# Loading the first group of q and k in fp32 over the hardware DMA queues, with the casts on VectorE and ScalarE

## Chip, cores, metric

One core of a Trainium2 chip. The metric is device time in microseconds (us) of one execution. A "span" is the same thing inside the trace, from the first to the last instruction; it is about 2 us shorter than the device time. A "fast run" is an execution that the record does not mark as slow (by its span and its granted clock, the share of the full TensorE clock that the records show); all timed runs here are fast ones, only the single run of no_norms is of unknown state.

## The reference

Cross-covariance attention over channels, followed by a gated feed-forward layer, all fp32. B, N, C = 4, 6016, 256; d_ff = 1536; tau = 1.

```python
qn = q / (np.linalg.norm(q, axis=1, keepdims=True) + 1e-06)
kn = k / (np.linalg.norm(k, axis=1, keepdims=True) + 1e-06)
s = kn.transpose(0, 2, 1) @ qn / tau          # [B, C, C], a sum over all N rows
a = softmax(s)
x = (v @ a).reshape(B * N, C)
out = (sigmoid(x @ w_gate) * (x @ w_val)) @ w_out
```

What matters here: the first output needs the scores `s` of batch 0, and these need every row of batch 0's q and k. Nothing of the main work can start before these 12.3 MB of fp32 have been read.

## The kernel before

q and k are read in groups of four row tiles (128 partitions x 4 x 256). GpSimd issues all loads, as DMAs that cast fp32 to bf16 on the way. Batch 0 has 11 full groups (0 to 10) and two small ones of two tiles and one tile, so that little is left to do after the last landing.

```python
def load_qk(b, t0, nt):
    tiles = []
    for name, src in (("q", q), ("k", k)):
        tl = qkpool.tile([P, TPC, C], BF16, tag=name, name=name + "_sb")
        nc.gpsimd.dma_start(out=tl[:, :nt, :], in_=rows(src, b)[:, t0 : t0 + nt, :])
        tiles.append(tl)
    qk[b, t0] = tiles
...
nc.scalar.preload_act_table(ACT.Sqrt)
for t0, nt in groups0[:2]:
    load_qk(0, t0, nt)
make_identity(nc, ident_bf)                   # GpSimd; cut: a second one, memsets on VectorE
for t0, nt in groups0[2:]:
    load_qk(0, t0, nt)
...
for g in range(last0 + 2):                    # the opening: batch 0's scores and norms
    if g <= last0:
        t0, nt = groups0[g]
        sq[g] = (squares(0, t0, nt, 0, nc.vector),
                 squares(0, t0, nt, 1, nc.vector if g == last0 else nc.scalar))
        for u in range(nt):
            score(0, t0, u)                   # 2 matmuls a tile: 8 for a full group
    if g >= 1:                                # column sums of the squares, 16 matmuls
        norm_mms(ps_n0, sq.pop(g - 1), groups0[g - 1][1], g == 1, g == last0 + 1)
```

After the loop come the norms, the softmax (with filler matmuls, `busy`, between them), the first products of the softmax with the weights (`ps_gh`), and then the main loop, whose first matmul is `ps_gate`.

## Time and profile before

| | before |
|---|---|
| median of the first three runs | 842.0 us (841.8 to 842.13) |
| the profiled run | 839.55 us |
| span in the trace | 837.4 us, TensorE busy 98% |
| first DMA bytes | between 2.5 and 2.6 us |
| scores of the last full group start | 32.22 us |
| first `ps_gate` matmul | 40.09 us |

The last two rows split the span: up to the last full group the DMA sets the pace, from there to `ps_gate` a chain of short steps on all engines, and after `ps_gate` TensorE. That last part is the same in every trace: span minus the start of the first `ps_gate` matmul is 797.2 to 797.6 us in all 14 of them. So whatever a variant does to the span is already visible at about 40 us.

### The profile page before, as it was taken

The page shows a single profiled execution, that of the slowest core. Times are in us where ns is not written, and L with a number is a line of the kernel's source. Part 1 is how long each engine was busy: PE and PEld are TensorE (multiplying, and loading weights), DVE is VectorE, ACT ScalarE, POOL GpSimd, SP SyncE. Part 2 cuts the span into 40 slices and gives each one's busy share as a digit, 9 for nine tenths or more (in the row PEclk, how much of TensorE's full clock was granted, in tenths as well). Part 3 has the DMA queues.
Part 4 walks back from the last instruction along what each step waited for, and adds up shares of the span by engine and source line. Part 5 has one row for each costly group of instructions (what it writes and reads, how often), then busy time and mean ns, then how long its engine had stood idle before and what let it go on. Part 6 is the DMA issues. An engine that isn't in the chain of part 4 may idle for free.

```text
span 837.4 us, 13986 instructions
## 1 busy us (share of the span) xinstructions
PE 816.6 (98%) x5327; PEld 506.3 (60%) x5338; DVE 565.3 (68%) x976; ACT 389.3 (46%) x639; POOL 83.9 (10%) x161
## 2 busy tenths in 40 slices
PE   5899999999999999999999999999999999999998
PEld 4546666665666666665566666666566565656666
DVE  2477777776667777777656777777766666666664
ACT  3554444446544444444554444444654444444442
POOL 5532100002011100000210020000000000000000
PEclk9899999999999999999999999999999999999999
DMA  9999624227655543223864353223222522322211
GB/s 176 206 206 188 131 51 89 61 51 142 119 102 107 101 108 63 48 51 89 150 136 86 88 117 78 51 76 67 58 48 51 95 51 76 76 48 68 48 35 69
DMA packets 78738, 76.65 MB, mean 92 GB/s; under 512 B 50768, under 2 KB 55632, under 8 KB 78672
## 3 DMA queue, kind: packets, MB, share of 16 engines
q0 software_dynamic: 24208, 39.33, 28.4%
q1 hardware_dynamic: 54464, 36.45, 15.8%
q8 instruction: 41, 0.67, 0.3%
q14 instruction: 25, 0.20, 0.1%
HBM read 78.64 MB, written 24.64 MB: 123 GB/s over the span
## 4 chain that ended last, share of the span: by engine, by line
PE 91%; DMA 3%; DVE 2%; ACT 1%; issue 1%; POOL 0%; ACTq 0%; POOLq 0%
PE ps_o L88 29%; PE ps_gate L88 28%; PE ps_val L88 28%; PE ps_s L88 4%; DMA k_sb<-in_k_dram 3%; PE ps_gh L88 2%; DVE hT L344 1%; ACT g_sb L343 1%; PE ps_rk L88 0%; ACT gh_H L299 0%; DVE out_sb L370 0%; PE ps_n L88 0%; DVE gh_G L301 0%; DVE gh_H L301 0%; DVE x_sb L246 0%
## 5 line engine op out<-in xcount | busy, mean ns | idle before, releaser
L344 DVE TENSOR_TENSOR hT<-ps_val,g_sb 128x512 bf16<-128x512 f32 (+1 forms) x576 | 390.9, 679 | 220.1 <-ACT g_sb L343 216.2
L343 ACT ACTIVATE g_sb<-ps_gate 128x512 bf16<-128x512 f32 (+1 forms) x576 | 338.6, 588 | 400.0 <-PE ps_gate L88 387.6
L88 PE MATMUL ps_val<-vT,gh_H 128*128 128x512 bf16 (+1 forms) x1152 | 338.1, 375 | 0.5
L88 PE MATMUL ps_gate<-vT,gh_G 128*128 128x512 bf16 (+1 forms) x1152 | 337.5, 375 | 0.5
L88 PE MATMUL ps_o<-w_out_sb,hT 128*128 128x256 bf16 x2256 | 326.1, 273 | 0.0
L88 PEld LDWEIGHTS <-hT 128*128 128x128 bf16 x2256 | 220.7, 98 | 124.8
L88 PEld LDWEIGHTS <-gh_H 128*128 128x128 bf16 x1152 | 112.7, 98 | 132.9 <-ACT gh_H L299 1.5
L88 PEld LDWEIGHTS <-gh_G 128*128 128x128 bf16 x1152 | 112.4, 98 | 37.3 <-ACT gh_G L299 0.3
L370 DVE COPY out_sb<-ps_o 128x256 f32<-128x256 f32 x188 | 78.0, 415 | 20.9 <-PE ps_o L88 20.9
L106 POOL DMA_DIRECT2D v_sb<-in_v_dram x48 | 25.5, 531 | 631.3 <-DMA vT<-v_sb 496.3
L88 PE MATMUL ps_s<-k_sb,q_sb 128*128 128x256 bf16 x376 | 72.3, 295 | 12.2 <-DMA k_sb<-in_k_dram 12.2
L88 PEld LDWEIGHTS <-q_sb 128*128 128x128 bf16 x376 | 39.1, 104 | 20.3 <-issue 7.5
L162 DVE TENSOR_TENSOR sq<-q_sb 128x1024 bf16<-128x1024 bf16 (+3 forms) x46 | 30.4, 661 | 25.3 <-PE ps_n L88 19.1
L200 DVE TENSOR_TENSOR acc<-acc,sq 128x1024 bf16<-128x1024 bf16 (+1 forms) x66 | 44.1, 669 | 0.0
L97 POOL DMA_DIRECT2D k_sb<-in_k_dram x49 | 26.9, 549 | 14.5 <-DMA k_sb<-in_k_dram 9.1
L97 POOL DMA_DIRECT2D q_sb<-in_q_dram x49 | 26.8, 548 | 13.7 <-DMA q_sb<-in_q_dram 6.3
L162 DVE TENSOR_TENSOR sq<-k_sb 128x1024 bf16<-128x1024 bf16 (+2 forms) x34 | 22.4, 658 | 0.0
L160 ACT ACTIVATE sq<-k_sb 128x1024 bf16<-128x1024 bf16 (+1 forms) x12 | 12.2, 1021 | 20.1 <-DMA k_sb<-in_k_dram 19.7
L88 PE MATMUL ps_gh<-w_gate,e_sb 128*128 128x512 bf16 x41 | 12.8, 378 | 1.6 <-DVE rrow L274 1.2
L88 PEld LDWEIGHTS <-e_sb 128*128 128x128 bf16 x112 | 9.9, 97 | 6.8 <-issue 3.2
L88 PE MATMUL ps_gh<-w_val,e_sb 128*128 128x512 bf16 x44 | 13.2, 379 | 0.4
L299 ACT ACTIVATE gh_G<-ps_gh,rrow 128x512 bf16<-128x512 f32 x12 | 8.2, 687 | 9.7 <-PE ps_gh L88 5.6
(44 smaller groups left out, 99.7 us busy)
## 6 DMA issues: line engine op xcount, KB each, us to landing
out_dram<-out_sb SPq DMA_DIRECT2D x44, 512.0 KB, 2.9
q_sb<-in_q_dram POOLq DMA_DIRECT2D x44, 256.0 KB, 6.7
k_sb<-in_k_dram POOLq DMA_DIRECT2D x44, 256.0 KB, 7.6
v_sb<-in_v_dram POOLq DMA_DIRECT2D x44, 256.0 KB, 3.9
out_dram<-out_sb SPq DMA_DIRECT2D x4, 384.0 KB, 2.4
w_gate<-in_moe_w_gate_dram POOLq DMA_DIRECT2D x3, 256.0 KB, 7.0
w_val<-in_moe_w_val_dram POOLq DMA_DIRECT2D x3, 256.0 KB, 7.6
w_out_sb<-in_moe_w_out_dram POOLq DMA_DIRECT2D x1, 768.0 KB, 13.0
```

Of the source, the lines that this page charges most:

```text
L88: nc.tensor.matmul(out, lhsT=lhsT, rhs=rhs, start=start, stop=stop, **kw)
L97: nc.gpsimd.dma_start(out=tl[:, :nt, :], in_=rows(src, b)[:, t0 : t0 + nt, :])
L106: nc.gpsimd.dma_start(out=v_sb[:, :nt, :], in_=rows(v, b)[:, t0 : t0 + nt, :])
L160: nc.scalar.activation(out=sq[:, :nt, :], in_=src[:, :nt, :], func=ACT.Square)
L162: engine.tensor_tensor(out=sq[:, :nt, :], in0=src[:, :nt, :], in1=src[:, :nt, :], op=ALU.mult)
L200: nc.vector.tensor_tensor(out=acc[:, :nt, :], in0=acc[:, :nt, :], in1=st[b]["sq", w][:, :nt, :], op=ALU.add)
L299: nc.scalar.activation(out=dst, in_=ps, func=ACT.Copy, scale=r)
L343: nc.scalar.activation(out=g_sb[:, :n], in_=ps_gate[:, :n], func=ACT.Sigmoid)
L344: nc.vector.tensor_tensor(out=hts[b, ci][:, f, :n], in0=ps_val[:, :n], in1=g_sb[:, :n], op=ALU.mult)
L370: nc.vector.tensor_copy(out=out_sb[:, s, :], in_=ps)
```

## The change

Intent: SP and ScalarE should be able to issue a DMA earlier than GpSimd does, and the first bytes should then move earlier. No cast is asked of these DMAs (the prediction says on what ground), so group 0 lands in fp32 tiles and is cast by VectorE (q) and ScalarE (k).

```diff
+    t0, nt = groups0[0]
+    qk[0, 0] = [qkpool.tile([P, TPC, C], BF16, tag=n, name=n + "_sb") for n in ("q", "k")]
+    first_f32 = [consts.tile([P, nt, C], FP32, name=f"first{w}") for w in range(2)]
+    for eng, tl, src in zip((nc.sync, nc.scalar), first_f32, (q, k)):
+        eng.dma_start(out=tl, in_=rows(src, 0)[:, t0 : t0 + nt, :])
     nc.scalar.preload_act_table(ACT.Sqrt)
-    for t0, nt in groups0[:2]:
-        load_qk(0, t0, nt)
+    load_qk(0, *groups0[1])
 ...
+    nc.vector.tensor_copy(out=qk[0, 0][0], in_=first_f32[0])
+    nc.scalar.copy(qk[0, 0][1], first_f32[1])
     for t0, nt in groups0[2:]:
         load_qk(0, t0, nt)
```

## The prediction

> **What bounds the kernel now.** I read the page first, then the chain of waits cut to the first 34 us, then the opening as a timeline, then stretches of it as a table. The page settles where a change to the opening can count at all. The chain that ended last is:
>
> ```profile
> PE 91%; DMA 3%; DVE 2%; ACT 1%; issue 1%; POOL 0%; ACTq 0%; POOLq 0%
> PE ps_o L88 29%; PE ps_gate L88 28%; PE ps_val L88 28%; PE ps_s L88 4%; DMA k_sb<-in_k_dram 3%; PE ps_gh L88 2%; DVE hT L344 1%; ACT g_sb L343 1%; PE ps_rk L88 0%; ACT gh_H L299 0%; DVE out_sb L370 0%; PE ps_n L88 0%; DVE gh_G L301 0%; DVE gh_H L301 0%; DVE x_sb L246 0%
> ```
>
> TensorE carries 91% of the span. The DMA share, 3% (about 27 us of 837.4), is the loading of batch 0's q and k, at the front. The chain cut to the opening shows that this is one unbroken wait for k:
>
> ```profile
> 5.06 6.56 DMA k_sb<-in_k_dram
> ...
> 11.91 10.48 DMA k_sb<-in_k_dram
> ...
> 22.67 9.51 DMA k_sb<-in_k_dram
> 32.18 0.04 issue
> 32.22 1.03 PE ps_s L88 x8
> ```
>
> Columns are start, length, what. The reader is to see that until 32.2 us the end is set by one thing, when the last full k group lands. From there on it is TensorE's own work, so a change of x us in that landing should pass almost undiminished to the end. Everything else in the opening has slack. The stretches show why the landing comes when it does (stretch, its length, busy time of PE, PEld, DVE, ACT and POOL, granted clock, DMA share, GB/s written):
>
> ```profile
> 2.25:2.50 0.25, 0.00 (x0) 0.00 (x0) 0.00 (x0) 0.00 (x0) 0.25 (x2) 1.00 0.00 0
> 2.50:2.75 0.25, 0.00 (x0) 0.00 (x0) 0.00 (x0) 0.00 (x0) 0.25 (x1) 1.00 1.30 82
> 2.75:3.00 0.25, 0.00 (x0) 0.00 (x0) 0.00 (x0) 0.00 (x0) 0.25 (x2) 1.00 1.15 57
> 3.00:3.25 0.25, 0.00 (x0) 0.00 (x0) 0.00 (x0) 0.00 (x0) 0.25 (x1) 1.00 0.61 41
> 3.25:3.50 0.25, 0.00 (x0) 0.00 (x0) 0.00 (x0) 0.00 (x0) 0.25 (x2) 1.00 0.42 57
> 3.50:4.00 0.50, 0.00 (x0) 0.00 (x0) 0.00 (x0) 0.00 (x0) 0.42 (x2) 1.00 0.95 164
> 4.00:4.50 0.50, 0.00 (x0) 0.00 (x0) 0.00 (x0) 0.00 (x0) 0.43 (x3) 1.00 1.11 209
> ```
>
> No data moves before 2.5 us, there is a weak first microsecond, and from 4.0 us on the engines are saturated. The 209 GB/s are bf16 bytes written; the sources are fp32, so they read 418 GB/s. A group of q and k is 2 x 512 KiB of fp32, so 1.049 MB / 418 GB/s = 2.51 us. The score matmuls of successive groups start at 9.22, 11.67, 14.23 and 16.67 us, 2.48 us apart: the rate of the source bytes sets the pace. The timeline of the first group:
>
> ```profile
> 1.23 0.66 POOL L97 DMA_DIRECT2D q_sb<-in_q_dram  x1 [0.78 <-POOLq L494]
> 5.43 0.69 DVE L162 TENSOR_TENSOR sq<-q_sb 128x1024 bf16<-128x1024 bf16 x1 [4.42 <-DMA q_sb<-in_q_dram]
> 6.63 1.06 ACT L160 ACTIVATE sq<-k_sb 128x1024 bf16<-128x1024 bf16 x1 [4.61 <-DMA k_sb<-in_k_dram]
> 6.65 1.86 PE L88 MATMUL ps_s<-k_sb,q_sb 128*128 128x256 bf16 x8 [6.65 <-DMA k_sb<-in_k_dram]
> ```
>
> q is issued at 1.23 us, its first bytes move at 2.5, it lands at 5.4, and k at 6.6.
>
> **What the Trainium skill says, and whether the trace agrees.** (1) "DMA: Bandwidth & Descriptors", section "SWDGE vs HWDGE vs iDMA": a DMA that casts must be issued from GpSimd; plain ones may go from SP or ACT. That is why the change needs an fp32 tile and two casts. Its Specifications give a first-byte latency of about 1 us for the GpSimd path and 0.6 us for the other. The trace has 1.27 us from the start of the first GpSimd issue to first bytes; for the hardware path it has only the output stores, 512 KB each, 2.9 us from issue to landing. (2) The same page, "Issuing engines are not separate DMA queues": all DMAs share 16 engines and interleave, so more issuers save issue time alone. The flat 209 GB/s agrees with one shared limit. (3) "VectorE: DVE Perf Modes", "The perf-mode tier table": an fp32 copy in SBUF runs at two elements a cycle, 1227 ns for 2048. An estimate from that page's fixed 150 cycles: (150 + 512) / 0.96 = 0.69 us for 1024. Nothing in the trace before is such a copy. (4) "ScalarE: Activation LUTs", "What ACT_TABLE_LOAD costs": 186 ns + 0.833 ns an element, 1.04 us for 1024; the trace's square of that size takes 1.06 us.
>
> **The change, part by part.** *Removed*: two GpSimd issues, 0.66 + 0.54 us, and group 0's 1.05 MB from the GpSimd queue. Group 1 takes its place at 1.23 us. GpSimd's issues (0.55 us for 1.25 us of transfer) run ahead of the data, so the saving there is worth nothing by itself.
>
> *Added, start of the stream*: SP and ACT issue at about 0.75 us (ACT's first instruction, the table load, starts at 0.74, so ACT is free then). An issue on SP takes 0.33 to 0.36 us in the trace, and a 512 KB store lands 2.9 us after it starts: less 1.25 us of transfer (0.524 MB / 418 GB/s) leaves 1.65 us, of which I put 0.85 ahead of the data and 0.8 behind, a choice. Data should therefore move from about 1.6 us in place of 2.5. What counts is the effective start at full rate. Before: k of group 0 landed at 6.63; less the 2.51 us for two tiles and an assumed 0.6 us of completion, 3.5 us. After: 1.6 us plus a weak spell as in the table (there 1.0 us) gives 2.6; a shorter one gives down to 2.1. The stream should thus end 0.9 to 1.4 us earlier; I take 1.1.
>
> *Added, the casts*: 0.69 us on VectorE and 1.04 us on ScalarE, beside each other. The three queues share the engines from about 2.6 us on, so group 0 loses its head start: of its 1.05 MB some 0.2 move by then, and 0.85 MB at two thirds of 418 GB/s take 3.0 us, plus completion 6.2 us at the latest; served alone, about 4.9. I take 5.9. ScalarE's cast then ends near 6.95, so the first score starts about 7.0, 0.3 us later than the 6.65 of before. This is not on the path that sets the end, for a group costs a slow TensorE about 2.27 us against 2.51 us of arrival (1.86 for scores plus 0.61 for norms, partly overlapped), and 1.57 when fast. A backlog under a microsecond is gone well before 32 us. ScalarE's square at 1.06 us and VectorE's at 0.69 us leave more slack.
>
> *Moved*: the table load falls behind ACT's issue, some 0.4 us, and its result is first needed at 35 us. The fp32 tiles take 8 KB a partition, no cost in time.
>
> *Sum*: the last full k lands at about 31.1 us in place of 32.2. Of the 1.1 us I expect to lose up to 0.2 because of TensorE's clock. These stretches are the reason:
>
> ```profile
> 17.90:24.60 6.70, 3.45 (x67) 3.05 (x65) 2.08 (x3) 2.11 (x2) 2.64 (x5) 0.99 1.12 210
> 24.70:31.40 6.70, 6.18 (x58) 4.53 (x58) 1.38 (x2) 3.17 (x3) 3.01 (x6) 0.51 1.12 208
> 31.60:38.00 6.40, 5.81 (x105) 5.09 (x102) 3.73 (x11) 4.01 (x6) 5.25 (x8) 1.00 1.24 204
> ```
>
> The granted clock is half from about 24.7 to 31.5 us and full just before the tail. If that change stays at the same moment, work that arrives at 31.1 runs for 0.4 us at half speed. The gain is then 0.9 to 1.1 us, and 842.0 becomes about 841.0.
>
> **Rivals.** *Nothing gained, the start was hidden*: if the hardware queues' first bytes were as late as GpSimd's, or the weak microsecond came from cold memory and were only moved, the total bytes would decide. For it: rates are equal on all queues, and the first stretches have packets in flight (share 1.30) with few bytes arriving. Against it: the share falls to 0.42 at 3.25 us, so the engines were short of work there, which a second source fills. Time: 842.0.
>
> *The cast becomes the bound*: the chain of landing, cast, square and score delays group 0 and this is never made up. For it: one cold group fills 2.27 of 2.51 us. Against it: the 17.9 to 24.6 stretch has 3.45 us of work in 6.7, so there is room to catch up. Time: 842.3 to 842.8.
>
> *The clock phases shift*: TensorE gets its full clock in one stretch and loses it in the next. A later start followed by denser work could move the half-clock stretch onto the tail, where from 32.2 to 38 us nearly all is TensorE or what waits for it. The eight scores took 1.86 us slow against 1.03 fast; over the tail that makes 2 to 3 us. For it: a half-clock stretch follows one with 51% work. Against it: the kernel puts filler matmuls (ps_busy) into the tail to prevent this. Time: 843 to 844. I give it one chance in eight.
>
> *More than I think*: if the loads start at full rate at once, the effective start is 1.6 us and the gain near 1.9: 840.1.
>
> **Range and chances.** The centre is 841.0. Below, 840.1 is the best rival; above, a lost phase makes 843.5. The chip's spread, 0.3 us in the three runs, is small beside these, but another chip may differ by a microsecond or so. I set 839.3 to 843.2 for eight times in ten. Two per cent is 16.8 us. The whole opening up to the last landing is 32 us and 27 of them are source bytes that must move either way, so no part of this change can win or lose that: same 0.985, faster 0.005, slower 0.01.
>
> **What would show each step right or wrong.** In the changed kernel's stretches, bytes should move by about 1.6 us. First score near 7.0 us, cast 0.7 us on VectorE and 1.04 on ScalarE. Later groups should be ready about 1.1 us earlier and 2.5 us apart, the scores after the last full k at about 31.1, and the first ps_gate matmul about 1 us before its 40.09 of before. I am wrong if the first bytes come at 2.5 us again, if TensorE no longer waits for k in the opening (the cast took over), if the tail runs at half clock, or if the last landing comes earlier but the end does not.

## The result, and the profile after

The changed kernel takes 839.42 us (838.86 to 840.19, 6 runs), the kernel before 841.4 us over its own 6 runs (839.72 to 842.13). Ratio 0.998, 95% interval 0.9967 to 0.9993, "same" at two per cent. Ratios here are the mean time of one kernel's fast runs over that of the other's of the same rounds, so not quite the ratio of the medians.

The first thing to see is a contradiction: the profiled run of the changed kernel has the *longer* span, 838.0 us against 837.4, although its runs are faster. Part of the answer is which executions were profiled: the trace before is of a run of 839.55 us, faster than all six timed runs (839.72 is the lowest), and the trace after is of the slowest of its six (840.19). The two traces must be taken apart before either is believed.

**The start went as hoped.** The timeline of the changed kernel (start, length, engine, instruction, in brackets the idle time before it and what ended it):

```profile
0.74 0.40 ACTq L114 DMA_DIRECT2D first<-in_k_dram  x1
0.74 0.39 SPq L114 DMA_DIRECT2D first<-in_q_dram  x1
1.23 0.67 POOL L97 DMA_DIRECT2D q_sb<-in_q_dram  x1 [0.78 <-POOLq L501]
5.54 0.69 DVE L127 CAST q_sb<-first 128x1024 bf16<-128x1024 f32 x1 [4.53 <-DMA first<-in_q_dram]
5.75 1.04 ACT L128 CAST k_sb<-first 128x1024 bf16<-128x1024 f32 x1 [3.29 <-DMA first<-in_k_dram]
6.84 3.57 PE L88 MATMUL ps_s<-k_sb,q_sb 128*128 128x256 bf16 x16 [6.84 <-ACT k_sb L128]
```

The loads go out 0.49 us ahead of GpSimd's first. The casts take 0.69 and 1.04 us, and the last line holds 16 matmuls, two groups in one piece: group 1 was already there when group 0 was done. In stretches (the last columns are granted clock, DMA share, GB/s written):

```profile
1.50:2.00 0.50, 0.00 (x0) 0.00 (x0) 0.00 (x0) 0.50 (x1) 0.50 (x2) 1.00 0.76 90
2.50:2.75 0.25, 0.00 (x0) 0.00 (x0) 0.00 (x0) 0.00 (x0) 0.17 (x2) 1.00 0.39 147
3.00:3.25 0.25, 0.00 (x0) 0.00 (x0) 0.00 (x0) 0.00 (x0) 0.18 (x3) 1.00 1.02 377
5.50:6.00 0.50, 0.00 (x0) 0.00 (x0) 0.46 (x1) 0.25 (x1) 0.50 (x2) 1.00 1.08 205
```

Bytes move in the stretch from 1.5 us. (The packet records have the first packet of q or k at 1.76 us, and at 2.59 in the kernel before.) While the fp32 tiles are written the rate shows as near 400 GB/s, as source and destination have the same size; at 5.5 us it is back at the 205 of casting DMAs. One thing went otherwise than predicted: GpSimd's loads of group 1 are issued at 1.23 us, as before, but their first packet moves at 4.97 us, when the fp32 loads are nearly done (their last packet ends at 5.34). In all eight traces with early hardware loads GpSimd's first packet comes at 4.80 to 5.29 us, in the others at 2.59 to 2.62. No run tests why. The engines are full at 3.0 us, where in the kernel before they were full at 4.0.

**A part of the lead is lost at group 6 in this pair of traces.** The score matmuls of groups 5, 6 and 7, first of the kernel before:

```profile
19.25 1.03 PE L88 MATMUL ps_s<-k_sb,q_sb 128*128 128x256 bf16 x8 [0.72 <-DMA k_sb<-in_k_dram]
...
22.43 1.03 PE L88 MATMUL ps_s<-k_sb,q_sb 128*128 128x256 bf16 x8 [1.77 <-DMA k_sb<-in_k_dram]
...
24.74 1.86 PE L88 MATMUL ps_s<-k_sb,q_sb 128*128 128x256 bf16 x8 [0.90 <-DMA k_sb<-in_k_dram]
```

and of the changed kernel:

```profile
18.22 1.75 PE L88 MATMUL ps_s<-k_sb,q_sb 128*128 128x256 bf16 x8 [1.11 <-DMA k_sb<-in_k_dram]
...
21.59 1.86 PE L88 MATMUL ps_s<-k_sb,q_sb 128*128 128x256 bf16 x8 [1.22 <-DMA k_sb<-in_k_dram]
...
24.14 1.54 PE L88 MATMUL ps_s<-k_sb,q_sb 128*128 128x256 bf16 x8 [0.28 <-DMA k_sb<-in_k_dram]
```

Group 5 is 1.03 us earlier than before. Group 6 comes late in both kernels (3.18 and 3.37 us after its predecessor, where 2.5 is the rule), and by group 7 the lead is 0.60 us. It stays there: the last full group starts at 31.61 against 32.22. Two checks show that the stream as a whole loses nothing. In the packet records 3 MB of the source have been read at 10.66 us before and 9.89 after, and 11 MB at 29.85 and 29.06: the lead is 0.77 and 0.79 us. (A casting DMA's packet records count bf16 bytes; they are doubled here.) And in the second pair of traces, below, the lead is 0.98 us at group 5 and 0.92 at group 9. What differs at group 6 is how late the last packet of a group comes.

**The tail is slower in this one trace.** The chain that ended last, from the last full group on, before:

```profile
32.22 1.03 PE ps_s L88 x8
33.26 0.38 PE ps_n L88 x16
33.63 0.52 PE ps_s L88 x4
...
40.25 0.43 PE ps_gate L88 x2
```

and after:

```profile
31.61 1.86 PE ps_s L88 x8
33.48 0.40 PE ps_n L88 x16
33.88 0.88 PE ps_s L88 x4
...
40.95 0.43 PE ps_gate L88 x2
```

The same eight score matmuls take 1.86 us, not 1.03, and the next four 0.88, not 0.52. From the last full group's scores to the first `ps_gate` matmul it takes 9.18 us (31.61 to 40.79) against 7.87 (32.22 to 40.09; the chain leaves out what overlaps the piece before, so it has `ps_gate` 0.16 us later than the timeline). The stretch says why:

```profile
31.60:38.00 6.40, 6.29 (x89) 5.23 (x89) 3.04 (x10) 3.31 (x5) 4.94 (x7) 0.70 1.24 205
```

The granted clock is 0.70 in it; before it was 1.00 (shown in the prediction). In this execution TensorE ran at half clock from 28.6 to 35.4 us. So the sum of this pair of traces is -0.61 us of stream and +1.31 us of tail, together the +0.7 us by which `ps_gate` starts later. Whether the change causes the slow tail or chance does is the question for the experiments.

### The profile page after: what moved, and what is told of

It is laid out like the page before. It is cut to its first block, busy times and chain, and to the rows that moved or that the text cites. A ratio compares the mean times of both kernels' runs of the same rounds, so it can differ in the third digit from the quotient of the medians.

```text
span 838.0 us, 14001 instructions
## 1 busy us (share of the span) xinstructions
PE 817.0 (97%) x5338; PEld 506.6 (60%) x5338; DVE 566.3 (68%) x977; ACT 390.6 (47%) x640; POOL 83.2 (10%) x159
## 4 chain that ended last, share of the span: by engine, by line
PE 91%; DMA 3%; DVE 2%; ACT 1%; issue 1%; POOL 0%; ACTq 0%; POOLq 0%
PE ps_o L88 29%; PE ps_gate L88 28%; PE ps_val L88 28%; PE ps_s L88 4%; DMA k_sb<-in_k_dram 3%; PE ps_gh L88 2%; DVE hT L351 1%; ACT g_sb L350 1%; PE ps_rk L88 0%; DVE out_sb L377 0%; ACT gh_H L306 0%; PE ps_n L88 0%; DVE gh_H L308 0%; DVE gh_G L308 0%; DVE x_sb L253 0%
## 5 line engine op out<-in xcount | busy, mean ns | idle before, releaser
L88 PEld LDWEIGHTS <-q_sb 128*128 128x128 bf16 x376 | 39.1, 104 | 20.8 <-issue 7.1
```

What stands on the lines that cost most here:

```text
L88: nc.tensor.matmul(out, lhsT=lhsT, rhs=rhs, start=start, stop=stop, **kw)
```

## The experiments

Theory A: the gain is the earlier start of the byte stream; the casts are hidden; where TensorE's half-clock stretches fall is chance, a matter of the single execution. Rivals: B, the change moves the clock's phase; C, the earlier stream is lost elsewhere; D (an addition to A), the late group is the work of an instruction fetch, a DMA packet that brings TensorE its next instructions; E, DMAs that don't cast, or the hardware queues as such (E'), are the gain; F, the casts cost; G, GpSimd's queue is the slow part.

Twelve kernels ran in three batches of four, each batch on a chip of its own. So times are compared within a batch, or by the ratio to the runs of the kernel before in the same batch. Their results are in one table. "First bytes" is the first packet of q or k in the packet records and "11 MB" the time at which 11 MB of the source have been read; "group 9" and "`ps_gate`" are the starts, in the trace, of that group's scores and of the first `ps_gate` matmul.

| batch | run | first bytes | 11 MB | group 9 | `ps_gate` | median us (lowest to highest of 5) | ratio to before |
|---|---|---|---|---|---|---|---|
| 0 | before | 2.59 | 29.85 | 29.75 | 40.09 | 841.4 (839.72 to 842.13, 6 runs) | |
| 0 | after | 1.76 | 29.06 | 29.15 | 40.79 | 839.42 (838.86 to 840.19, 6 runs) | 0.9980 |
| 1 | before_copy | 2.60 | 29.88 | 30.11 | 40.44 | 839.99 (839.87 to 841.54) | 0.9991 |
| 1 | after_copy | 1.76 | 28.98 | 29.19 | 40.00 | 839.40 (838.98 to 840.22) | 0.9984 |
| 1 | fill_before | 2.59 | 30.00 | 30.18 | 40.90 | 840.19 (840.03 to 840.36) | 0.9990 |
| 1 | fill_after | 1.75 | 29.10 | 29.23 | 39.88 | 839.04 (839.00 to 839.29) | 0.9977 |
| 2 | wide_before | 2.59 | 29.83 | 29.97 | 40.87 | 840.37 (839.91 to 840.48) | 0.9994 |
| 2 | wide_after | 1.75 | 29.04 | 29.25 | 39.60 | 838.83 (838.63 to 839.39) | 0.9979 |
| 2 | wide_pool_f32 | 2.62 | 29.92 | 30.22 | 40.60 | 839.84 (839.44 to 840.33) | 0.9989 |
| 2 | wide_act_late | 1.77 | 29.08 | 29.54 | 39.87 | 838.91 (838.76 to 839.32) | 0.9978 |
| 3 | wide_late_hw | 2.60 | 29.97 | 30.01 | 40.92 | 840.00 (839.49 to 840.20) | 0.9983 |
| 3 | wide_cast_twice | 1.75 | 29.03 | 29.06 | 40.03 | 839.21 (839.13 to 839.71) | 0.9976 |
| 3 | wide_two_groups | 1.76 | 29.11 | 29.14 | 40.05 | 839.56 (839.26 to 839.84) | 0.9979 |
| 3 | no_norms | 1.75 | 28.98 | 28.37 | 40.19 | 839.57 (1 run) | |

The column "11 MB" falls into two sets: 28.98 to 29.11 us wherever the first bytes come at 1.75 to 1.77, and 29.83 to 30.00 wherever they come at 2.59 to 2.62. In both sets it hardly depends on who issues, on casts, or on fillers.

### The two kernels again (before_copy, after_copy)

No edit. The kernel before:

> The kernel before against itself, for the noise and for a second trace of it. Theory A (the half-clock stretch of TensorE falls at a different phase in each run, and the two profiles of before and after differ in the tail only by that): the runs' mean granted clocks are not all 0.996; they spread over 0.990 to 0.997 and the spans over some 1.5 us; in this trace the scores of the last full group start at 32.2 us within 0.3 us, whatever the clock. Rival B (the phase follows the kernel and the change moved it): all runs near 0.996 and the half-clock stretch again at 24.7 to 31.5 us. Ratio 1.000 either way.

And the changed one:

> The changed kernel again, for a second trace and a clean ratio. Theory A: k of group 1 is ready near 8.2 us (1.0 us before the kernel before), last full group's scores at 31.2 to 31.6 us, the tail at full or half clock by chance; ratio 0.9985 to 0.9995 (0.4 to 1.3 us). Rival B: the half-clock stretch is again at 28.6 to 35.4 us, so the tail from the last full group's scores to the first ps_gate matmul takes 9.3 us again against 8.0 of before, and the ratio is 1.000 to 1.001.

The copy of the kernel before measured 0.9991 of the kernel before (interval 0.9979 to 1.0004): the same program, and the medians of five and nine runs differ by 1.0 us. That is the size of the effect looked for, so plain timing of these kernels hardly resolves it. The clock moved: in the copy of before the half-clock stretch reaches from 21.4 to 31.6 us (24.4 to 31.3 in the first trace), in the copy of after the later of two lies at 26.0 to 32.8 (28.6 to 35.4 in the first). Rival B, a phase that the kernel fixes, is out. That the change makes a bad phase likelier is not excluded by two traces of each, but the runs show no sign of it: the mean granted clock is 0.992 both over 32 runs of the kernel before and over 11 of the changed one. The tails follow the clock: 7.85 us in the copy of before (32.59 to 40.44), 8.35 us in that of after (31.65 to 40.00) with the half clock covering its first microsecond. The mean granted clocks of the before runs in this batch go from 0.987 to 0.996, so they spread, as A expects, even a little further. One part missed: the last full group of the copy starts at 32.59, 0.37 us off the first trace, just outside the 0.3 I had allowed. It is not the stream: 11 MB are read within 0.03 us of each other, and up to group 5 (19.25 and 19.22) the traces agree. They part at group 6 (22.43 and 22.57), behind the fetch at 20.2 us, which costs the one 0.5 us for good and the other 0.9. In the copy of after the last full group starts at 31.65, and the ratio is 0.9984, each just outside its expected range.

### TensorE kept busy (fill_before, fill_after)

```diff
+    busy(48)                                   # 128 columns each
     for g in range(last0 + 2):
         if g <= last0:
+            if 1 <= g and groups0[g][1] == TPC:
+                busy(12)
```

> The kernel before with filler matmuls on TensorE while it waits: 48 ahead of the first group and 12 ahead of each full group from the second on. Takes the clock's phase out of the comparison. Theory A: granted clock 1.00 from about 6 us through the tail, last full group's scores at 32.2 us as before (the fillers lie in DMA waits), tail 8.0 us, time within 0.5 us of before and the spread of the runs smaller. Rival B': the fillers come to bound the opening in place of the DMA, scores of the last full group later than 32.5 us, time up by 0.5 us or more.

> The changed kernel with the same fillers. Theory A: last full group's scores at 31.1 to 31.6 us, tail 8.0 us at full clock, so the first ps_gate matmul at 39.1 to 39.6 us; faster than fill_before by 0.6 to 1.1 us (ratio to before 0.9985 to 0.9993), and never slower than after_copy. Rival C (the earlier stream is lost elsewhere whatever the clock): the same time as fill_before within 0.3 us.

With the fillers the granted clock is full through the tail in both traces, and the scatter collapses: 840.03 to 840.36 and 839.00 to 839.29, a third of a microsecond each, where before and its copy scatter over 1.7 to 2.0 us and after and its copy over 1.2 to 1.3. This fits a scatter made mostly by the clock's phase, but does not isolate it: the fillers move the instruction fetches too, and runs of the kernel before with the same mean clock of 0.992 still have spans from 838.0 to 839.7 us. With the scatter out of the way, the change is worth 840.21 - 839.10 = 1.1 us in the means, with no overlap of the runs. `ps_gate` starts 1.02 us earlier. A holds, C falls. Both traces have their fetches at the same places (13.05, 23.37 and 31.99 us in fill_before, each 0.8 to 1.0 us sooner in fill_after), so this is the cleanest pair. The misses: the third fetch delays the small group 11 (its scores wait for DMA until 34.33 us in fill_before and 33.21 in fill_after), so the tail took 8.28 and 8.16 us and not 8.0. The last full groups start at 32.62 and 31.72 us, each a little too late: two late groups lie before them, not one. The 32.62 is past the mark of B', yet TensorE still waits for k there and the time did not rise, so B' is out. And fill_before is 0.8 us faster than before, not within 0.5.

### Fewer filler instructions (wide_before, wide_after)

```diff
+    ones_wide = consts.tile([P, CH], BF16)      # 512 columns
+    nc.vector.memset(ones_wide, 1.0)
 ...
-    busy(48)
+    busy_wide(12)                               # 512 columns each
-                busy(12)
+                busy_wide(3)
```

> The kernel before with the same filler time in a quarter of the instructions (512 columns each: 12 ahead of the first group, 3 ahead of each full one). Theory D: what makes one k group come 0.7 to 0.9 us late in every trace so far is a 16 KB instruction fetch, whose packet holds one DMA engine for 0.97 us: before the fetch at 20.3 us the group 6, with narrow fillers fetches at 13.1, 23.4 and 32.0 us and groups 3, 7 and 11. With wide fillers the first fetch comes later than 13.1 us, at most one before the last full group, and the time is 0.3 to 0.7 us below fill_before (839.5 to 839.9). Rival: the lateness has another cause, the gaps stay at groups 3 and 7, time as fill_before (840.2).

> The changed kernel with wide fillers. Theory A with D: full clock in the tail, 0.9 to 1.2 us faster than wide_before, so 838.3 to 838.9, the fastest so far. Rival C: the same as wide_before within 0.3 us.

The change is again worth over a microsecond: 840.28 - 838.96 = 1.3 us in the means, no overlap. The expected time of D, 839.5 to 839.9 us, failed: wide_before is no faster than fill_before. Its traces say why. Fetches come at 17.7 and 31.0 us, the groups that follow (5 and 10) start late, and the second one now strikes the last full group, whose scores start at 33.06. So D's account of the late groups held and its sum did not: spreading the same fillers over fewer instructions only moved the second fetch onto a worse place. wide_after has the lowest median, 838.83 us, 0.9979 of before, within the noise of fill_after. Some of the 1.3 us is the fetch's place and not the stream: wide_after's second fetch, at 30.36 us, leaves its last full group alone (31.71). Of the 1.27 us between the two `ps_gate` starts, 0.72 are there at group 9 and the rest arises at the last full group.

### No hardware queue (wide_pool_f32)

```diff
-    for eng, tl, src in zip((nc.sync, nc.scalar), first_f32, (q, k)):
+    for eng, tl, src in zip((nc.gpsimd, nc.gpsimd), first_f32, (q, k)):
```

> As wide_after, but group 0's fp32 loads are issued by GpSimd: the fp32 tiles and the two casts stay, the hardware queues and the earlier issue go. Theory A (the whole gain is the earlier start of the stream, the casts are hidden): first bytes at 2.5 us, first scores at about 7.7 us, group 1 ready at 9.2 us, time equal to wide_before within 0.25 us. Rival E (the gain comes from DMAs that don't cast): time equal to wide_after. Rival F (the casts cost): 0.5 us or more slower than wide_before.

First bytes at 2.6 us, group 0's scores at 7.67 us as expected. Lines of wide_before, then of this run, for group 9:

```profile
29.97 1.03 PE L88 MATMUL ps_s<-k_sb,q_sb 128*128 128x256 bf16 x8 [0.46 <-DMA k_sb<-in_k_dram]
```

```profile
30.22 1.03 PE L88 MATMUL ps_s<-k_sb,q_sb 128*128 128x256 bf16 x8 [0.46 <-DMA k_sb<-in_k_dram]
```

The later groups come no earlier than in wide_before, so tiles without a cast in the DMA gain nothing in the stream (rival E), and the casts cost at most the 0.25 us between these two lines (F). The time, 839.84, is 0.5 us below wide_before and 1.0 above wide_after. That is outside the 0.25 us expected. In its trace `ps_gate` comes 0.27 us sooner than in wide_before, though group 9 came 0.25 later: wide_before's last full group is hit by the fetch at 31.0 us and this one's is not (32.69, the fetch comes at 31.36). It is the fetch's luck rather than the edit's merit, on one trace's evidence.

### One hardware queue (wide_act_late), an edit that missed its aim

```diff
+    nc.scalar.preload_act_table(ACT.Sqrt)
-    for eng, tl, src in zip((nc.sync, nc.scalar), first_f32, (q, k)):
+    for eng, tl, src in zip((nc.scalar, nc.scalar), first_f32, (q, k)):
 ...
-    nc.scalar.preload_act_table(ACT.Sqrt)
```

> As wide_after, but both fp32 loads are issued by ScalarE behind its table load, at about 2.0 and 2.4 us, so on a hardware queue yet without the head start over GpSimd. Theory A: first bytes at 2.5 us from GpSimd's group 1, the hardware queue only fills the weak microsecond after it; of the gain of wide_after at most half is left, time 0.1 to 0.5 us below wide_before. Rival E' (hardware queues as such make the opening shorter): the whole gain stays, time within 0.2 us of wide_after.

It kept the whole gain (838.91), as E' said, but it does not test what it was made for: the trace has ScalarE's loads at 0.77 and 1.17 us, *beside* its table load (0.73 to 2.01), not behind it. So its agreement with E' decides nothing. What it does show is that one hardware queue does as well as two, in time and at 11 MB (29.08 against 29.04 us); its group 9 is 0.29 us later than in wide_after.

### The loads held back (wide_late_hw)

```diff
+    scratch = consts.tile([P, 512], FP32)
+    nc.vector.memset(scratch, 0.0)
+    nc.vector.memset(scratch, 1.0)
+    for tl in first_f32:
+        nc.vector.memset(tl[:, 0, 0:1], 0.0)     # the loads wait for these
     for eng, tl, src in zip((nc.sync, nc.scalar), first_f32, (q, k)):
```

> What wide_act_late was meant to test and did not (its loads went out at 0.77 and 1.17 us, ahead of the table load): wide_after with the two hardware-queue loads held back to about 2.1 us by memsets of VectorE that they depend on. Theory A (the earlier start is the gain): first bytes at 2.5 us, from GpSimd's group 1, hardware bytes from 2.9 us; at most half the gain left, 839.3 to 840.2 us. Rival E' (a hardware queue filling the ramp is the gain, not its early issue): within 0.25 us of wide_after, 838.6 to 839.1.

This is the decisive one: the hardware queues, the fp32 tiles, the casts and GpSimd's shorter list are all there, and the early issue is gone. The loads go out at 2.10 us and the first bytes are GpSimd's, none before 2.6 us. Those of the hardware queues come only at 4.66 us, not at 2.9 as expected, so group 0's scores start at 10.82 us; TensorE works without a wait from there and waits for k again from group 9 on. Group 9, here and then in wide_after:

```profile
30.01 1.03 PE L88 MATMUL ps_s<-k_sb,q_sb 128*128 128x256 bf16 x8 [0.45 <-DMA k_sb<-in_k_dram]
```

```profile
29.25 1.03 PE L88 MATMUL ps_s<-k_sb,q_sb 128*128 128x256 bf16 x8 [0.46 <-DMA k_sb<-in_k_dram]
```

0.76 us later than wide_after and level with wide_before (29.97), with one fetch before group 9 in each of the three; 11 MB are read at 29.97 us against 29.04 and 29.83. The gain of the stream is gone in the trace. (`ps_gate` at 40.92 says less: the fetch at 31.05 us hits the last full group here, as in wide_before and not in wide_after.) The times alone would not decide it. The median, 840.00, is the slowest of its batch by 0.4 to 0.8 us and lies in A's range and not in that of E', but these ranges came from another chip, its runs overlap with those of the two other timed kernels of the batch, and its ratio to before, 0.9983, is nearer to wide_after's 0.9979 than to wide_before's 0.9994, all with intervals of about 0.0013 to either side.

### The casts doubled (wide_cast_twice)

```diff
     nc.vector.tensor_copy(out=qk[0, 0][0], in_=first_f32[0])
     nc.scalar.copy(qk[0, 0][1], first_f32[1])
+    nc.vector.tensor_copy(out=qk[0, 0][0], in_=first_f32[0])
+    nc.scalar.copy(qk[0, 0][1], first_f32[1])
```

> wide_after with each of the two casts done twice: 0.7 us more on VectorE and 1.04 us more on ScalarE ahead of group 0. If the casts are hidden: group 0's scores at 7.9 us in place of 6.9, group 4's again at 15.7 to 15.9 us, time within 0.25 us of wide_after (838.6 to 839.1). Rival F (the casts are on the path): 0.7 us or more slower.

```profile
8.09 1.03 PE L88 MATMUL ps_s<-k_sb,q_sb 128*128 128x256 bf16 x8 [1.33 <-ACT k_sb L132]
...
29.06 1.03 PE L88 MATMUL ps_s<-k_sb,q_sb 128*128 128x256 bf16 x8 [0.46 <-DMA k_sb<-in_k_dram]
```

Group 0 waits 1.2 us longer for ScalarE (8.09 against 6.87), group 4 is already back in step (15.86 against 15.71), and group 9 is no later. (`ps_gate` is 0.43 us later than in wide_after, as the fetch, at 30.16 us, hits the last full group, 32.23. That is not the casts' doing: wide_two_groups, without doubled casts, has the same fetch at 30.18 and the same delay, 32.26.) The median of 839.21 is a little above the range I had written from another chip; the ratio to before, 0.9976 against wide_after's 0.9979, shows no cost. F is out.

### Two groups over the hardware queues (wide_two_groups)

```diff
-    t0, nt = groups0[0]
+    for t0, nt in groups0[:2]:                   # fp32 tiles and loads for both
 ...
-    load_qk(0, *groups0[1])
+    load_qk(0, *groups0[2])                      # and the casts moved into the loop, g < 2
```

> wide_after with groups 0 and 1 both loaded in fp32 over the hardware queues and cast. Theory A: the stream starts at 1.5 us as before and is full at 3.0, nothing more to win: time within 0.25 us of wide_after. Rival G (GpSimd's queue is the slower one, so each group taken from it gains about a microsecond): 0.6 us or more faster than wide_after.

No further gain: group 9 at 29.14 us, 11 MB at 29.11, ratio 0.9979, the same as wide_after. (The plain median is 0.73 us above wide_after's, on another chip and with the last full group hit by a fetch.) Within its batch it is 0.35 us above wide_cast_twice. Once the stream has started, who issues the rest does not matter. G is out.

### Fewer TensorE instructions in the opening (no_norms)

```diff
         if g >= 1:
-            norm_mms(ps_n0, sq.pop(g - 1), groups0[g - 1][1], g == 1, g == last0 + 1)
+            sqs = sq.pop(g - 1)
+            if g in (1, last0, last0 + 1):
+                norm_mms(ps_n0, sqs, groups0[g - 1][1], g == 1, g == last0 + 1)
```

(The result is wrong by 3.8%: the norms lack most groups.)

> The changed kernel without fillers and, wrong on purpose, without the norm matmuls of groups 1 to 10, which takes some 300 TensorE instructions out of the opening. Theory D: the first instruction fetch comes after 30 us, no gap between the scores of successive full groups is over 2.7 us, and the last full group's scores start at 30.6 to 30.9 us in place of 31.6. Rival: one gap of 3.3 us is still there near 20 us and the last full group again starts at 31.4 us or later.

In the queue table of the kernel before, the stretch from 20.0 to 20.8 us has this line; from 10 to 19 us there is none:

```profile
q8 instruction: 1, 0.02, 7.6%
```

One packet of 16 KB; the packet records give it 0.975 us, from 20.27 us on. In no_norms the only one before 50 us comes at 29.62, and the late group has moved with it:

```profile
25.80 1.86 PE L88 MATMUL ps_s<-k_sb,q_sb 128*128 128x256 bf16 x8 [1.41 <-DMA k_sb<-in_k_dram]
28.37 1.87 PE L88 MATMUL ps_s<-k_sb,q_sb 128*128 128x256 bf16 x8 [0.70 <-DMA k_sb<-in_k_dram]
31.80 3.14 PE L88 MATMUL ps_s<-k_sb,q_sb 128*128 128x256 bf16 x14 [1.56 <-DMA k_sb<-in_k_dram]
```

Groups 6 to 9 now come every 2.44 to 2.57 us, so that group 9 is 0.78 us earlier than in the changed kernel, and it is group 10 that comes 3.43 us after its predecessor. My numbers missed (I had put the fetch after 30 us and hence the last full group at 30.6 to 30.9), but the mechanism is shown: the instruction count decides when the fetch comes, and the group in flight then is late. (That the packet holds up one of the 16 DMA engines is read from its length; the traces kept don't say which engine a packet ran on. The single run's time proves nothing.)

## Why the prediction was right or wrong

The measured 839.42 us lies in the range of 839.3 to 843.2, though 0.12 us from its lower edge, and "same" was right. By its own steps:

- **What sets the end up to 32 us.** Right. The part behind the first `ps_gate` matmul is constant to 0.4 us in 14 traces.
- **Earlier start of the stream: first bytes at 1.6 in place of 2.5 us, 1.1 us in the landings.** Right in kind, a little too large. Bytes move from 1.76 us in place of 2.59; groups 2 to 5 start 1.0 us earlier (group 5: 18.22 against 19.25), and the sum of bytes is 0.8 us ahead all along. The cause is shown and not only argued: holding back the issue (wide_late_hw) takes the gain of the stream away. (A slip of reading: the hardware path carries SP's transposes too in the trace before, not only stores, and GpSimd's first bytes come 1.36 us after its issue, not 1.27.)
- **Casts of 0.69 and 1.04 us, group 0's scores at 7.0 us, hidden.** Right: 0.69, 1.04 and 6.84, the casts as the prediction had estimated them. Doubling them costs nothing in the stream. That k landed near the 5.9 us taken (ScalarE's cast starts at 5.75) is partly luck: the step let three queues share the engines from 2.6 us on, but GpSimd's first packet moved at 4.97, so the fp32 loads ran nearly alone.
- **The last full k at 31.1 us.** Wrong by half a microsecond: its scores start at 31.61 us. The step took the 1.1 us to hold to the end of the stream. An instruction fetch, which I had not looked for although the kernel before shows its gap at group 6, costs either kernel 0.5 to 0.9 us of a group's landing, and its size varies. In the four pairs of before and after the lead at group 9 is 0.60, 0.92, 0.95 and 0.72 us.
- **TensorE's clock: at most 0.2 us lost, if the change to full clock stays at its moment.** The condition was wrong. The moment moves from run to run for either kernel. (In the trace before, the half clock ends at 31.28 us by the clock's records, not at 31.5.) The third rival (phases shift onto the tail) is what the profiled run shows, +1.31 us, yet, as far as the copies show, as chance and not as an effect of the change. I gave it one chance in eight as if it were decided once; it is drawn anew in each execution.
- **The centre, 841.0 us.** Too high by 1.6 us. About 0.6 of that is the base: 842.0 was the median of three runs at the upper end of a scatter whose six runs have a median of 841.4. The rest is in the noise of the ratio (0.998 is 1.7 us, with an interval from 0.6 to 2.8). The two pairs with fillers give 1.1 and 1.3 us for the change, close to the predicted 1.0; the second holds some luck with a fetch.

What stays open: why a fetch of the same size costs 0.5 us in one execution of the kernel before and 0.9 in another (this is the 0.37 us between before and before_copy at the last full group), how much of the scatter in time is the clock and how much the fetches, and why GpSimd's first packets wait when the hardware loads go first.

## What to carry to other kernels

When an opening is bound by a saturated DMA stream, look first at when the stream starts: here first bytes 0.83 us sooner put the stream 0.8 to 0.9 us ahead to its end, while who issued a second group, or another microsecond of casts, was of no account. Below half a per cent, don't subtract two single traces: keep the clock up with filler matmuls in the waits, or compare the stages and the bytes moved, so that chance in one stage is not taken for the effect of a change in another. And look at what else uses the DMA engines: instruction fetches ride with the data.

## What the Trainium skill lacked or had wrong

- **"DMA: Bandwidth & Descriptors", section "Issuing engines are not separate DMA queues"** says that DMAs of all issuing engines share 16 engines, but not what an instruction fetch among them costs a load stream that fills them. Here each fetch is one 16 KB packet of 0.89 to 0.98 us, and every trace has a load group that came 0.6 to 1.5 us late behind one; cutting instructions moved it (no_norms: from 19.2 to 29.6 us).
- **Same page, Specifications**: first-byte latency of 0.6 us on the hardware path and about 1 us on GpSimd's. Measured from the start of the issue to the first packet: 1.02 us (0.74 to 1.76) and 1.36 us (1.23 to 2.59). The lead of about 0.4 us roughly agrees (0.34), the values don't, though the page doesn't say from which moment it counts; the rest of the head start is GpSimd's later issue.
- **"TensorE: Matmul & The Clock Gate", section "What's actually happening"**: an activity window of 3413 ns that runs free and doesn't reset with the kernel. The traces agree: the half-clock stretches of the opening last 3.41, 6.83 or 10.24 us and lie elsewhere in each execution. What the page lacks is a figure for a tuned kernel that waits for DMA in its opening: runs scattered over 1.2 to 2.0 us in 840, and with fillers over 0.3 to 0.9 (how much of that is the clock is not separated here).
- **No page that I read** says that a DMA issued by ScalarE need not wait for the table load ahead of it: in wide_act_late it went out at 0.77 us, 0.04 us after the load had started.
